# A fixed table for the opening of a windowed-attention and feed-forward kernel

## The chip, the cores and the metric

The kernel runs on one core of a Trainium2 chip. A core has five engines with queues of their own, which run at the same time and wait for one another through semaphores: TensorE (PE in the profile; PEld is its loading of weights), VectorE (DVE), ScalarE (ACT), GpSimd (POOL) and SyncE (SP, which here only issues DMAs). Every engine takes its instructions strictly in the order in which they stand in its queue. The metric is the device time of one execution in microseconds, the median of several runs. Lower is better.

## The reference

Two stages follow each other. The first is attention in a window over q, k, v of shape (8 batches, 8 heads, 576 positions, 64). The first four heads of a batch see the 32 latest positions, the other four every fourth of the 128 latest.

```python
scores = scale * np.matmul(q, k.transpose(0, 1, 3, 2))
mask_plain = (rel >= 0) & (rel < window)
mask_dil = (rel >= 0) & (rel < window * dilation) & (rel % dilation == 0)
scores = np.where(masks[None, :, :, :], scores, -1000000000.0)
scores = scores - np.max(scores, axis=-1, keepdims=True)
attn = np.exp(scores)
attn = attn / (np.sum(attn, axis=-1, keepdims=True) + 1e-09)
return np.matmul(attn, v).astype(np.float32)
```

Its result, seen as 4608 tokens by 512, goes through a feed-forward stage with weights 512 x 2048 and 2048 x 512.

```python
h = x @ w_in
relu6 = np.clip(h + 3.0, 0.0, 6.0)
g = h * relu6 / 6.0
return (g @ w_out).astype(np.float32)
```

All inputs are fp32, and the result is wanted to fp32's accuracy. So the kernel takes each fp32 operand of the feed-forward products apart into a rounded high part and a rest, and makes three products of them: high by high, high by rest, rest by high.

## The kernel before

**Attention in trios.** The work of the attention is cut into 48 trios. One trio is 192 positions of four heads, whose scores fill one 128x384 tile: every block of 32 queries meets only its own 32 keys and the 32 before it. The first 12 trios (two batches) are all done at the start and in a form of their own. For such a trio, TensorE adds the mask as a product (line 228) and 24 small score products (line 163, two passes each, so 48 matmuls in the trace); VectorE takes the row maxima and subtracts them (195, 196); ScalarE takes the exponential (200); TensorE turns the tile in three transposes (242), ScalarE copies it out of PSUM (245); TensorE multiplies by the values (line 173, again 48 matmuls), VectorE divides by the sums (207, 208, 210), TensorE turns again (242), ScalarE copies (247), and ScalarE and GpSimd write the high part xh (299) and the rest xl (302) of the feed-forward's input. The score products of a trio and the value products of the trio three before it are issued alternately, in one block of 96 matmuls. The other 36 trios are spread over the later feed-forward steps and turn by VectorE and DMAs.

**Feed-forward in steps.** The tokens are cut into 12 chunks of 384, the 2048 hidden units into 16 parts of 128. One step (chunk c, part f) is gemm1 (lines 397 to 418: 12 matmuls of 384 columns into a ps_h tile, then Relu, gate, high part and rest on ScalarE and VectorE in turn) and, two steps later, gemm2 (420 to 434: 9 matmuls of 512 columns into three ps_o tiles, which stay in PSUM while f runs). That makes 192 steps. Chunks 0 and 1 run interleaved so that each converted weight is used twice when it is new; LEAD says by how many steps chunk 0 is ahead.

**Weights.** The 16 parts come as 32 halves of 512 KB (an even half belongs to w_in, an odd one to w_out), and each is converted on the chip: two products on ScalarE (338, 339), three steps on VectorE (340, 346, 350), the high part on ScalarE (351), the rest on VectorE (355). The input says them as 64-bit words, hence the work on single bits. A pool of 18 slots of 8 KB per partition holds 16 converted parts, and in what is left the halves that are being converted; the inputs of trios 0 to 8 also lie there at first (the name first).

**What sets the order.** In the kernel before, the code hands work to a scheduler that orders each engine's queue, TensorE's too, by priorities and by a simulated time: step n has priority n, the evaluation of its first product n - 1.9, gemm2 n + 0.8, the rest between; constants such as CB, EARLY and WITH say beside which trio a conversion, a step or a load is handed over. SP's queue holds at most eight loads in flight: from the ninth on, each waits for the landing of the one eight before it.

Of the kernel before, what the change touches and what calls it, by code (L numbers as in the profile page):

```python
# [25 lines left out]
BEATS = 30  # L26
EXTRA = 2
WARM = 8
ONV = ()
AHEAD = 3  # L30
LEAD = 4
# [3 lines left out]
WITH = (0, 0, 0, 0, 2, 0, 2, 0, 2, 2, 2, 2)  # L35
CB = (6, 6, 7, 7, 8, 8, 9, 9, 10, 10, 11, 11, 12, 12)
BASE = 8
CD = 0.5
EARLY = (8, 9, 10, 11, 12, 13, 14, 15, 15)
# [3 lines left out]
NEG = -1.0e30  # L43


@with_exitstack
def windowed_attention_ffn(ctx: ExitStack, tc: tile.TileContext, qk, vp, w, mask, out):
# [73 lines left out]

    last = {}
    kqs, vs = {}, {}
# [11 lines left out]
    def load_qk(t):  # L135
        if t < T and t not in kqs:
            kqs[t] = load_tile(t, "kq", 0, KW + CH)
            nc.sync.dma_start(out=kqs[t], in_=qk[t].rearrange("h d x -> (h d) x"))
# [7 lines left out]
    es, ats, xs, xfs = {}, {}, {}, {}  # L146
    trios = _order(B)
# [10 lines left out]
    def mm_scores(t, ps, i, u, r, masked):  # L158
# [4 lines left out]
        last["pe"] = nc.tensor.matmul(  # L163
# [5 lines left out]
    def mm_values_first(t, ps, i, u, h):  # L169

        k, j = divmod(i, 2)
        rows, n, at, s = slice(j * D, (j + 1) * D), 4 * k + 2 * (1 - h) + u, QB * (2 * j + u), 2 * k + h
        last["pe"] = nc.tensor.matmul(
            ps[at : at + QB, s * W : (s + 1) * W],
            lhsT=ats[t][rows, QB * n : QB * (n + 1)], rhs=vs[t][rows, 4 * k + 2 * h + u, :], start=True, stop=True,
        )

    def mm_values(t, ps, i, u, r):

        rows, n, at = slice(r * D, (r + 1) * D), SLOTS * u + i, QB * (2 * (1 - r) + u)  # L180
        last["pe"] = nc.tensor.matmul(  # L181
# [4 lines left out]
    def softmax(t, ps, masked):  # L186
        e = work_tile("e")
        mx = small.tile([P, SLOTS], F32, name="mx")
        ev = e.rearrange("p (s x) -> p s x", x=2 * QB)
        sv = ps[:, :CH].rearrange("p (s x) -> p s x", x=2 * QB)  # L190
        if not masked:
            _, kind, part = trios[t]
            nc.vector.tensor_tensor(out=e, in0=ps[:, :CH], in1=mask_sb[:, 3 * kind + part], op=ALU.add)
            sv = ev
        nc.vector.tensor_reduce(out=mx, in_=sv, axis=AX.X, op=ALU.max)
        nc.vector.tensor_tensor(  # L196
            out=ev, in0=sv, in1=mx.rearrange("p (s o) -> p s o", o=1).broadcast_to([P, SLOTS, 2 * QB]),
            op=ALU.subtract,
        )
        nc.scalar.activation(e, e, AF.Exp, scale=SCALE)  # L200
        es[t] = e
        load_qk(t + NLOAD)

    def normalise(t, ps):
        pv = ps[:, : SLOTS * W].rearrange("p (s x) -> p s x", x=W)
# [9 lines left out]
        xs[t] = x  # L215
        load_v(t + NLOAD)
# [4 lines left out]
    def st_both(ts, tv):  # L221
# [7 lines left out]
        for i, u, r in blocks():  # L229
            if tv is not None:  # L230
                (mm_values_first if tv < NFIRST else mm_values)(tv, pv, i, u, r)
            if ts is not None:
                mm_scores(ts, ps, i, u, r, masked)
        if tv is not None:
            normalise(tv, pv)
        if ts is not None:
            softmax(ts, ps, masked)

    def turn(src, name):
# [3 lines left out]
        dst = work_tile(name)  # L243
        if name == "a":
            nc.scalar.copy(dst, ps[:, :CH])
        else:
            nc.scalar.copy(
                dst.rearrange("p (u i x) -> p i u x", u=2, x=QB),
                ps[:, :CH].rearrange("p (i u x) -> p i u x", u=2, x=QB),
            )  # L250
        return dst
# [18 lines left out]
    def st_turn_e(t, how):  # L270
        ats[t] = how(es.pop(t), "a")

    def st_turn_x(t, how):
        xfs[t] = how(xs.pop(t), "xf")

    def st_split(t):
        xf = xfs.pop(t)

        b, kind, part = trios[t]
        assert all(read[c] == NF for c in chunks(b - 2, kind, part))  # L280
        written.add((b, kind, part))
        xu = xf.rearrange("p (u f) -> p u f", u=2)
        half = CH // 2
        to = lambda x: x[:, 2 * kind : 2 * kind + 2, b % 2 * S : b % 2 * S + S]
        pieces = []
        if kind == 0:
            pieces.append((xu, lambda x: to(x)[:, :, half * part : half * (part + 1)]))
        else:
            at = half * part
            while at < half * (part + 1):  # L290
                c, i0 = divmod(at, CLS)
                n = min(CLS - i0, half * (part + 1) - at)
                pieces.append((
                    xu[:, :, at - half * part : at - half * part + n],
                    lambda x, c=c, i0=i0, n=n: to(x).rearrange("p u (i c) -> p u c i", c=DIL)[:, :, c, i0 : i0 + n],
                ))
                at += n
        for src, view in pieces:
            nc.scalar.copy(view(xh), src)  # L299
        for src, view in pieces:  # L300
            eng = nc.vector if t in ONV else nc.gpsimd
            eng.tensor_tensor(out=view(xl), in0=src, in1=view(xh).bitcast(F32), op=ALU.subtract)  # L302
# [3 lines left out]
    def pace(ins):  # L306

        if "pe" in last:
            tc.add_manual_dep(
                ins.ins, last["pe"].ins.name,  # L310
                mybir.DependencyInfo(mybir.DependencyClass.NoSync, mybir.DependencyReason.DATA), reason="pace",
            )
# [5 lines left out]
    wt, staged = {}, {}  # L318
    WN = w.shape[3]

    def load_w(p):
        st = wpool.tile([P, 4, WN], F32, name="st", tag="w")
        pace(nc.sync.dma_start(
# [4 lines left out]
    def parts(p):  # L328
        st = staged[p]
        f, j = divmod(p, 2)  # L330
# [284 lines left out]
```

## Time and profile before

| what | value |
|---|---|
| median of 3 runs | 915.96 us (915.54 to 918.5) |
| profiled execution | 915.34 us, of which its span is 913.57 us |
| TensorE busy over the span | 891.0 us, 98% |
| VectorE, ScalarE, GpSimd busy | 444.0, 346.5, 62.5 us |
| mean granted TensorE clock | 0.991 |
| first matmul of a feed-forward step starts | 34.2 us |
| TensorE without any gap | from 100.3 us to 909.0 us |

The span is the time from the first to the last instruction. In the profile a matmul's end is modelled and matmuls overlap, so a row's mean duration is longer than the distance at which such matmuls follow each other; distances are read from starts. "Idle before" is time in which the engine had nothing under way ahead of an instruction, with the instruction or DMA that ended it; "issue" stands there if nothing that the profile records ended it.

### The profile page before, as it was taken

Reading aid. Unit: us, or ns where it says so; the run is one execution under the profiler, and the core shown is the slowest. Engines: PE = TensorE matmul, PEld = TensorE weight load, DVE = VectorE, ACT = ScalarE, POOL = GpSimd, SP = SyncE. Lnnn points to the kernel's source line nnn. Section 1 sums busy time; section 2 is a strip of 40 time slices with the busy share of each in tenths; the row PEclk is TensorE's granted clock in tenths of the full one; section 3 lists DMA queues with packets and bytes.
Section 4 is the critical chain, followed back from the end, with each engine's and each line's share of the span. In section 5 each row is a group of like instructions: output and inputs, shape, how many; then the busy total and the mean of one; then the engine's idle time right before and its main releaser. Section 6 shows DMA issues by size and latency. Waiting matters only on the chain.

```text
span 913.6 us, 20574 instructions
## 1 busy us (share of the span) xinstructions
PE 891.0 (98%) x8732; PEld 791.6 (87%) x8732; DVE 444.0 (49%) x934; ACT 346.5 (38%) x661; POOL 62.5 (7%) x77
## 2 busy tenths in 40 slices
PE   6897999999999999999999999999999999999998
PEld 4576999989889899899888989988888998899996
DVE  3899983244545454444454445445444544422221
ACT  2778862333333333233333223233333332332322
POOL 0212100000010110000000000000100010000000
PEclk9799999999999999999999999999999999999999
DMA  9927430022313222222122123113211310100000
GB/s 354 386 83 260 140 93 0 1 95 89 86 54 119 72 70 81 66 67 84 47 85 85 48 64 104 51 46 99 71 49 52 116 32 11 45 5 1 36 1 34
DMA packets 37820, 74.87 MB, mean 82 GB/s; under 512 B 7264, under 2 KB 16608, under 8 KB 37728
## 3 DMA queue, kind: packets, MB, share of 16 engines
q1 hardware_dynamic: 32544, 64.12, 21.8%
q10 hardware_dynamic: 5184, 9.44, 2.7%
q8 instruction: 68, 1.11, 0.5%
q14 instruction: 24, 0.20, 0.1%
HBM read 57.02 MB, written 9.44 MB: 73 GB/s over the span
## 4 chain that ended last, share of the span: by engine, by line
PE 92%; DMA 4%; DVE 2%; ACT 1%; issue 0%; SPq 0%; POOL 0%
PE ps_o L428 15%; PE ps_h L407 15%; PE ps_h L409 14%; PE ps_h L408 14%; PE ps_o L429 14%; PE ps_o L430 14%; PE ps_a L181 3%; PE ps_a L163 2%; DMA first<-in_v 2%; DMA st<-in_w 1%; DMA v<-in_v 1%; DVE st L350 1%; DVE st L346 1%; DVE wt L355 0%; PE ps_a L242 0%
## 5 line engine op out<-in xcount | busy, mean ns | idle before, releaser
L413 DVE SCALAR_TENSOR_TENSOR t<-t,ps_h 128x384 f32<-128x384 f32 x192 | 106.3, 554 | 326.0 <-ACT t L412 325.8
L407 PE MATMUL ps_h<-xh,wt 128*128 128x384 f32 x768 | 261.5, 341 | 2.9 <-DVE t L413 2.8
L408 PE MATMUL ps_h<-xl,wt 128*128 128x384 f32 x768 | 259.9, 338 | 0.5 <-POOL xl L302 0.5
L409 PE MATMUL ps_h<-xh,wt 128*128 128x384 f32 x768 | 259.9, 338 | 0.0
L428 PE MATMUL ps_o<-wt,gh 128*128 128x512 f32 x576 | 228.7, 397 | 2.0 <-ACT gh L416 2.0
L429 PE MATMUL ps_o<-wt,gh 128*128 128x512 f32 x576 | 224.9, 390 | 0.0
L430 PE MATMUL ps_o<-wt,gl 128*128 128x512 f32 x576 | 221.3, 391 | 0.6 <-DVE gl L417 0.6
L412 ACT ACTIVATE t<-ps_h,three 128x384 f32<-128x384 f32 x192 | 111.1, 579 | 273.3 <-PE ps_h L409 273.0
L417 DVE TENSOR_TENSOR gl<-t,gh 128x384 fp32r<-128x384 f32 x192 | 107.0, 557 | 101.4 <-ACT gh L416 100.1
L407 PEld LDWEIGHTS ps_h<-xh,wt 128*128 128x128 f32 x768 | 144.9, 189 | 11.8 <-DVE t L413 3.3
L408 PEld LDWEIGHTS ps_h<-xl,wt 128*128 128x128 f32 x768 | 144.9, 189 | 8.7 <-POOL xl L302 0.6
L409 PEld LDWEIGHTS ps_h<-xh,wt 128*128 128x128 f32 x768 | 145.0, 189 | 0.8 <-issue 0.3
L416 ACT CAST gh<-t 128x384 fp32r<-128x384 f32 x192 | 98.5, 513 | 111.3 <-DVE t L413 109.1
L430 PEld LDWEIGHTS ps_o<-wt,gl 128*128 128x128 f32 x576 | 108.2, 188 | 24.2 <-DVE gl L417 1.0
L428 PEld LDWEIGHTS ps_o<-wt,gh 128*128 128x128 f32 x576 | 108.3, 188 | 20.1 <-ACT gh L416 2.3
L429 PEld LDWEIGHTS ps_o<-wt,gh 128*128 128x128 f32 x576 | 108.4, 188 | 15.7
L302 POOL TENSOR_TENSOR xl<-xf,xh 128x384 fp32r<-128x384 f32 (+3 forms) x72 | 62.2, 877 | 740.6 <-ACT xh L299 671.8
L200 ACT ACTIVATE e<-e 128x384 f32<-128x384 f32 x48 | 25.2, 526 | 112.4 <-DVE e L196 112.3
L163 PE MATMUL ps_a<-kq 64*32 64x64 f32 x1872 | 47.1, 225 | 0.0
L299 ACT CAST xh<-xf 128x384 fp32r<-128x384 f32 (+3 forms) x72 | 33.7, 536 | 34.7 <-DMA xf<-xf_t 34.6
L181 PEld LDWEIGHTS ps_a<-v,a 64*32 64x32 f32 x1728 | 35.8, 105 | 9.2 <-issue 8.6
L181 PE MATMUL ps_a<-v,a 64*32 64x65 f32 x1728 | 41.6, 225 | 0.0
(45 smaller groups left out, 494.6 us busy)
## 6 DMA issues: line engine op xcount, KB each, us to landing
st<-in_w SPq DMA_DIRECT2D x32, 512.0 KB, 5.7
kq<-in_qk SPq DMA_DIRECT2D x39, 416.0 KB, 4.5
v<-in_v SPq DMA_DIRECT2D x39, 390.0 KB, 3.5
out<-o ACTq DMA_DIRECT2D x36, 256.0 KB, 2.9
first<-in_qk SPq DMA_DIRECT2D x9, 416.0 KB, 8.0
first<-in_v SPq DMA_DIRECT2D x9, 390.0 KB, 8.5
a<-a_t SPq DMA_DIRECT2D x144, 24.0 KB, 1.8
xf<-xf_t SPq DMA_DIRECT2D x144, 24.0 KB, 1.8
```

Source lines behind the costliest of these rows:

```text
L163: last["pe"] = nc.tensor.matmul(ps[at : at + QB, 2 * QB * i : 2 * QB * (i + 1)], lhsT=x[rows, KW + QB * n : KW + QB * (n + 1)], rhs=x[rows ...
L181: last["pe"] = nc.tensor.matmul(ps[at : at + QB, i * W : (i + 1) * W], lhsT=ats[t][rows, QB * n : QB * (n + 1)], rhs=vs[t][rows, n, :], st ...
L407: nc.tensor.matmul(ph, lhsT=wt[f][:, 0, ks], rhs=a, start=(kt == 0), stop=False)
L408: nc.tensor.matmul(ph, lhsT=wt[f][:, 0, ks], rhs=b, start=False, stop=False)
L409: last["pe"] = nc.tensor.matmul(ph, lhsT=wt[f][:, 1, ks], rhs=a, start=False, stop=(kt == NK - 1))
L412: nc.scalar.activation(t, ph, AF.Relu, bias=three, scale=1.0)
L413: nc.vector.scalar_tensor_tensor(out=t, in0=t, scalar=6.0, in1=ph, op0=ALU.min, op1=ALU.mult)
L416: nc.scalar.copy(gh, t)
L417: nc.vector.tensor_tensor(out=gl, in0=t, in1=gh.bitcast(F32), op=ALU.subtract)
L428: nc.tensor.matmul(po[c][tt], lhsT=gh[:, ts], rhs=wt[f][:, 2], start=(f == 0), stop=False)
L429: nc.tensor.matmul(po[c][tt], lhsT=gh[:, ts], rhs=wt[f][:, 3], start=False, stop=False)
L430: last["pe"] = nc.tensor.matmul(po[c][tt], lhsT=gl[:, ts], rhs=wt[f][:, 2], start=False, stop=(f == NF - 1))
```

## The change

The opening (the first 12 trios, all 32 halves of weights, and the first 28 feed-forward steps) is no longer handed to the scheduler with priorities. Its operations are listed in a table of names, ORDER, and issued in that order on ScalarE, VectorE and SyncE; for TensorE the whole program is now issued in the order of the code. For this, the functions that did several engines' work are cut into one function for each operation, and a letter names each: B a block of products (scores of trio t, values of trio t - 3), V values alone, R maxima, S subtraction, X exponential, E and Y the two turnings, CA and CX their copies, Z the division, XH and XL high part and rest, U Q s j a h l the seven operations of converting a half, k v w M loads, G and H the two products of a step, RE T GH GL its evaluation.

Other parts of it: xl of the first 12 trios is made on VectorE (before: GpSimd). LEAD is 2 (before 4). The two products of a step are whole, with no other product between them. The step after which trio 12 begins lies one step later. After the table, steps are handed over as before, with the conversion taken out. Loads of k and v also stand inside S and Z (`load_qk(t + NLOAD)`, `load_v(t + NLOAD)`), so a load can be issued there before its own name comes up in the table.

```diff
-LEAD = 4
+LEAD = 2
...
+FOLLOW = 3
+ORDER = """
+M1 k0 M0 k1 w0 B0 k2 B1 R0 w2 S0 U0 R1 k3 X0 s0 Q0 B2 S1 v0 j0 X1 E0 U2 R2 v2 E1 CA0 a0 Q2 w4 S2 h0 s2 B3 X2 l0 k5
+CA1 j2 k7 E2 a2 CA2 Z0 k4 U4 Q4 R3 B5 v1 h2 s4 S3 k6 j4 X3 Y0 R5 E3 CX0 v3 Z2 CA3 B4 XH0 w1 S5 XL0 X5 k9 a4 Y2 E5 R4
+CX2 B6 v4 CA5 Z1 XH2 w5 S4 h4 Y1 XL2 U1 R6 w3 X4 CX1 Z3 E4 Q1 v5 S6 CA4 Y3 XH1 l4 B7 v6 X6 XL1 CX3 l2 U3 k8 E6 s1
...
+    def shifted(t):
+        sv, mx = pss.pop(t)
         nc.vector.tensor_tensor(
...
+            in1=mx.rearrange("p (s o) -> p s o", o=1).broadcast_to([P, SLOTS, 2 * QB]), op=ALU.subtract,
+        )
         load_qk(t + NLOAD)
...
-            eng = nc.vector if t in ONV else nc.gpsimd
+    def low(t, eng):
+        for src, view in pieces_of(t):
             eng.tensor_tensor(out=view(xl), in0=src, in1=view(xh).bitcast(F32), op=ALU.subtract)
...
+        "B": lambda t: block(t, t - FOLLOW if t >= FOLLOW else None),
+        "V": lambda t: block(None, t),
...
+        "XH": high, "XL": lambda t: low(t, nc.vector),
...
-    place(-5, lambda: st_both(NFIRST, None))
-    place(-3, lambda: st_turn_e(NFIRST, turn_by_blocks))
+    place(-3, lambda: st_both(NFIRST, None))
+    place(-1, lambda: ats.update({NFIRST: turn_by_blocks(es.pop(NFIRST), "a")}))
...
+    with tc.manual_schedule(
+        engines={mybir.EngineType.Activation, mybir.EngineType.DVE, mybir.EngineType.SP}
+    ):
+        for name in ORDER.split():
+            kind = name.rstrip("0123456789")
+            first_operations[kind](int(name[len(kind) :]))
...
-        windowed_attention_ffn(tc, *args, o)
+        with tc.manual_schedule(engines={mybir.EngineType.PE}):
+            windowed_attention_ffn(tc, *args, o)
```

Where the instructions now stand, at three places. First TensorE's queue at the first product of step 0. Before, the products of step 0 (ps_h, lines 407 to 409) stand one by one between value products (line 173) and score products (163) of a block:

```order
L242 MATMUL ps_a<-ident,x 128x128 x3
L228 LDWEIGHTS mi
L228 MATMUL ps_a<-mi 128x384
L407 MATMUL ps_h<-xh,wt 128x384
L173 MATMUL ps_a<-first,a 32x65
L408 MATMUL ps_h<-xl,wt 128x384
L163 MATMUL ps_a<-first 32x64
L409 MATMUL ps_h<-xh,wt 128x384
L173 MATMUL ps_a<-first,a 32x65
L407 MATMUL ps_h<-xh,wt 128x384
L163 MATMUL ps_a<-first 32x64
```

Now (line 187 is a score product, 197 a value product, 285 a transpose, 432 to 434 the first product of a step):

```order
L197 MATMUL ps_a<-first,a 32x65
L187 MATMUL ps_a<-first 32x64
L285 MATMUL ps_a<-ident,e 128x128 x3
L432 MATMUL ps_h<-xh,wt 128x384
L433 MATMUL ps_h<-xl,wt 128x384
L434 MATMUL ps_h<-xh,wt 128x384
L432 MATMUL ps_h<-xh,wt 128x384
L433 MATMUL ps_h<-xl,wt 128x384
```

The 12 matmuls of step 0 stand together, behind the blocks of trios 0 to 9; before, they began in the block of trio 8's scores and were spread over that one and the next.

Second, SyncE's queue of loads at the values of trios 4 and 6 (first_106 and first_112 before, first_203 and first_365 now; st is a half of weights, kq the queries and keys of a later trio). Before:

```order
L138 DMA first_112<-in_qk 128x832
L144 DMA first_106<-in_v 128x780
L323 DMA st_115<-in_w 128x1024
L323 DMA st_117<-in_w 128x1024
L138 DMA first_119<-in_qk 128x832
L144 DMA first_109<-in_v 128x780
L138 DMA first_122<-in_qk 128x832
L144 DMA first_112<-in_v 128x780
```

Now:

```order
L161 DMA first_365<-in_qk 128x832
L167 DMA first_229<-in_v 128x780
L371 DMA st_442<-in_w 128x1024
L161 DMA first_445<-in_qk 128x832
L161 DMA kq_449<-in_qk 128x832
L167 DMA first_203<-in_v 128x780
L371 DMA st_526<-in_w 128x1024
L371 DMA st_540<-in_w 128x1024
L167 DMA first_365<-in_v 128x780
```

The values of trio 4 are the 22nd load (the 14th before), those of trio 6 the 25th (the 20th before); the first halves of weights have gone ahead of them, as have the values of trio 5 (first_229) and the keys of trios 8 and 9.

Third, the making of xl. Before, on GpSimd:

```order
L302 TENSOR_TENSOR xl<-xf,xh 128x2x192 x2
L302 TENSOR_TENSOR xl<-xf,xh 128x2x144
L302 TENSOR_TENSOR xl<-xf,xh 128x2x48
L302 TENSOR_TENSOR xl<-xf,xh 128x2x96 x2
L302 TENSOR_TENSOR xl<-xf,xh 128x2x48
```

Now in VectorE's queue, between the conversion of weights (393, 413), the softmax (219, 224) and the division (236 to 239):

```order
L224 TENSOR_TENSOR e<-ps_a,mx 128x384
L413 TENSOR_TENSOR wt<-st,wt 128x512
L343 TENSOR_TENSOR xl<-xf,xh 128x2x192
L413 TENSOR_TENSOR wt<-st,wt 128x512
L393 TENSOR_SCALAR st<-st 128x512
L236 TENSOR_SCALAR z<-ps_a 128x6
L237 RECIPROCAL z<-z 128x6
L239 TENSOR_TENSOR x<-ps_a,z 128x384
L219 TENSOR_REDUCE mx<-ps_a 128x6
L343 TENSOR_TENSOR xl<-xf,xh 128x2x96 x2
```

The 18 operations of the first 12 trios have moved from GpSimd to VectorE; those of the other 36 trios are still on GpSimd.

More of the change, by code (lines that the diff above doesn't have):

```diff
@@ L119, in windowed_attention_ffn, with in_turn @@
     nc.gpsimd.memset(three, 3.0)
+    kqs, vs = {}, {}
     last = {}
-    kqs, vs = {}, {}
+    def in_turn(ins):
+        for name in last.values():
+            tc.add_manual_dep(
+                ins.ins, name, mybir.DependencyInfo(mybir.DependencyClass.NoSync, mybir.DependencyReason.DATA), reason="in turn"
+            )
     wide = {}
@@ L268, in turn_by_blocks, with pieces_of @@
         return dst
[L270 to L277, printed above, removed]
+    def pieces_of(t):
+        b, kind, part = trios[t]
+        xu = xfs[t].rearrange("p (u f) -> p u f", u=2)
+        half = CH // 2
+        to = lambda x: x[:, 2 * kind : 2 * kind + 2, b % 2 * S : b % 2 * S + S]
+        if kind == 0:
+            return [(xu, lambda x: to(x)[:, :, half * part : half * (part + 1)])]
+        found, at = [], half * part
+        while at < half * (part + 1):
+            c, i0 = divmod(at, CLS)
+            n = min(CLS - i0, half * (part + 1) - at)
+            found.append((
+                xu[:, :, at - half * part : at - half * part + n],
+                lambda x, c=c, i0=i0, n=n: to(x).rearrange("p u (i c) -> p u c i", c=DIL)[:, :, c, i0 : i0 + n],
+            ))
+            at += n
+        return found
@@ L279, in st_split, with high @@
+    def high(t):
         b, kind, part = trios[t]
         assert all(read[c] == NF for c in chunks(b - 2, kind, part))
[L281 to L297, printed above, removed]
@@ L298, in st_split @@
-        for src, view in pieces:
+        for src, view in pieces_of(t):
             nc.scalar.copy(view(xh), src)
-        for src, view in pieces:
-            eng = nc.vector if t in ONV else nc.gpsimd
+    def low(t, eng):
+        for src, view in pieces_of(t):
             eng.tensor_tensor(out=view(xl), in0=src, in1=view(xh).bitcast(F32), op=ALU.subtract)
[L306 to L312, printed above, removed]
@@ L318, in windowed_attention_ffn, with st_split @@
-    wt, staged = {}, {}
+        xfs.pop(t)
+        written.add(trios[t])
+    def st_split(t):
+        high(t)
+        low(t, nc.gpsimd)
+    steps = [(0, f) for f in range(LEAD)]
+    for f in range(NF):
+        if f + LEAD < NF:
+            steps.append((0, f + LEAD))
+        steps.append((1, f))
+    steps += [(c, f) for c in range(2, NCH) for f in range(NF)]
+    when = {f: steps.index((0, f)) for f in range(NF)}
+    wt, staged, converted = {}, {}, set()
     WN = w.shape[3]
@@ L482, in step_at @@
             step()
-        turn_of(n + 0.4)
-        if LEAD <= n < BEATS:
-            convert_beat()
         turn_of(n + G2)
-        if n >= LAG:
-            gemm2(*steps[n - LAG])
+        if n - LAG not in done:
+            gemm2(n - LAG)
         turn_of(n + DEL + 0.5)
```

283 lines of the change are left out of this document (136 added, 147 removed).

## The prediction

> **What bounds the kernel now.** I read the span on the page first, then busy time by stage, then the groups of TensorE's instructions up to 100.28 us, then what TensorE waits for.
>
> ```profile
> span 913.6 us, 20574 instructions
> ...
> 50.60:100.30 49.70, 44.35 (x549) 36.80 (x550) 49.19 (x97) 42.50 (x86) 11.44 (x10) 0.97 0.56 189
> 100.30:909.10 808.80, 808.71 (x7318) 729.17 (x7316) 365.50 (x776) 277.24 (x525) 43.08 (x54) 1.00 0.19 59
> ...
> L407 PE MATMUL ps_h<-xh,wt 128*128 128x384 f32 x36 | 14.3, 401 | 2.9 <-DVE t L413 2.8
> ...
> L428 PE MATMUL ps_o<-wt,gh 128*128 128x512 f32 x21 | 8.9, 423 | 2.0 <-ACT gh L416 2.0
> ```
>
> The rows of the stages are busy us of PE, PEld, DVE, ACT, POOL with counts, then clock, DMA share and GB/s. From 100.3 us on TensorE is never idle at full clock, and the change leaves that work as it is: there is nothing to gain behind 100.3 us. TensorE's queue is the same there but for the place of a block by part of a product; only trio 12 is turned one step, 4.1 us, ahead of its values, against two before, for which two turnings on VectorE (under 1 us) and a transfer of 1.8 us (rows below) leave room; without it, 1 us at most. The last two rows are of the first 100.28 us: 36 matmuls of line 407 at 4 a step and 21 of line 428 at 3 a step are 9 first and 7 second products, beside the 12 trios. In 50.6 to 100.3 us VectorE is busy for 49.19 of 49.70 us, so it sets the pace there. What sets the first 50 us is in TensorE's waits:
>
> ```profile
> PE ps_a L173 <- issue: 9.3, 4, 3.8
> ...
> 31.98 0.21 PE L173 MATMUL ps_a<-first,a 64*32 64x65 f32 x1 [3.42 <-issue]
> ...
> 13.30:19.60 6.30, 2.47 (x127) 1.96 (x127) 1.75 (x5) 1.00 (x2) 0.00 (x0) 0.98 1.03 410
> 19.60:25.80 6.20, 5.34 (x126) 4.12 (x127) 3.50 (x10) 2.85 (x7) 1.00 (x1) 0.74 1.03 406
> 25.80:31.90 6.10, 2.69 (x127) 2.17 (x127) 4.73 (x11) 4.72 (x10) 1.00 (x1) 1.00 1.03 406
> ...
> q8 instruction: 68, 1.11, 0.5%
> ```
>
> Four times, 9.3 us in all and 3.8 at the longest, TensorE waits for "issue", which is nothing recorded; the wait that ended at 31.98 us is one. The next rows are three stretches from one such wait's end to the next. From each such wait to the next lie 127 matmuls and 127 weight loads, some 254 instructions, and 6.1 to 6.3 us, while the DMA engines are full (share 1.03). The instruction queue carries 68 packets, 1.11 MB: 16 KB each. I read this as a refill of TensorE's instructions: on entering one block of some 255 the next is sent for, and with the load stream full it comes 6.2 us later.
>
> **Prices of TensorE's work.**
>
> ```profile
> 57.32 0.81 PE ps_a L242 x6
> ...
> 108.03 0.68 PE ps_o L430 x3
> 112.15 0.68 PE ps_o L430 x3
> ...
> 349.21 0.43 PE ps_o L428
> ...
> 367.07 0.43 PE ps_o L428
> ...
> 64.17 0.34 PE L228 MATMUL ps_a<-mi 128*128 128x384 bf16 x1
> 64.44 0.26 PE L163 MATMUL ps_a<-kq 64*32 64x64 f32 x4
> ```
>
> From the chain of waits (start, us; the last two rows are TensorE's timeline): a step takes 112.15 - 108.03 = 4.12 us, 2.06 for each product. Four steps and a later trio take 17.86 us, so a block of 96 small matmuls is 17.86 - 16.5 = 1.35 us. Three transposes are 0.4 us, the mask 0.27 us (64.17 to 64.44). A block of scores and values is then 1.62 us, scores alone about 1.0, values alone 0.75.
>
> **When step 0 can begin.** In the table, the scores of trios 0 to 9 and the values of trios 0 to 6 come ahead of G0. Two paces meet there. First the loads:
>
> ```profile
> 10.22 8.35 DMA first<-in_v
> ...
> 18.58 9.14 DMA st<-in_w
> ...
> st<-in_w SPq DMA_DIRECT2D x32, 512.0 KB, 5.7
> ...
> v<-in_v SPq DMA_DIRECT2D x39, 390.0 KB, 3.5
> ...
> first<-in_qk SPq DMA_DIRECT2D x9, 416.0 KB, 8.0
> first<-in_v SPq DMA_DIRECT2D x9, 390.0 KB, 8.5
> ...
> xf<-xf_t SPq DMA_DIRECT2D x144, 24.0 KB, 1.8
> mi<-in_mask SPq DMA_DIRECT2D x1, 384.0 KB, 6.6
> mi<-in_mask SPq DMA_DIRECT2D x1, 224.0 KB, 2.7
> ```
>
> From the chain, then the DMA issues with KB each and us to landing. Before, the 14th load is issued at 10.22 us, when the 6th has landed, and lands 8.35 us later; the 22nd is issued at 18.58 and lands at 27.72 us. By the KB of the rows, 2246, 5470 and 9130 KB have come by 10.20, 18.57 and 27.72 us. By the new order, v0 ends at 4102 KB (15.0 us), k5 at 5420 KB (18.4), v1 at 6616 KB (21.4), v4 at 9156 KB (27.8), v6 at 10570 KB (at 400 KB/us, 31.3). By loads alone the block of trio 9's scores and trio 6's values begins at 31.3, the next follows, and G0 stands 1.62 + 1.62 + 0.4 later, at 35.0 us.
>
> Second the refills. Each matmul counts twice (its weight load): warm-up 16, scores alone 98, a block 194, three transposes 6. Block ends lie at about 190, 446, 702, 958, 1214, 1470 and 1726; G0 begins at 1748. Walking the table, with 6.2 us from entering a block to having the next:
>
> - 190, in B1 (k1 ends at 1440 KB, about 8.1 us), is passed at 9.1; the next block is there at 15.3.
> - 446 lies in B3, which waits for v0 until 15.0; passed at 15.9, next there at 22.1.
> - 702 lies at the end of B5 (k5, 18.4); reached at 19.7, waits to 22.1; next at 28.3.
> - 958 is early in B6; 3.6 us of B4 and turnings bring it to 25.8; waits to 28.3; next at 34.5.
> - 1214 is a third into B7; reached at 31.5; waits to 34.5; next at 40.7.
> - 1470 lies in B9; reached at 38.0 (Y4 waits for the division); waits to 40.7.
> - 1726 ends B8, reached at 42.9. The loads issued without a wait (to v8, 13596 KB) have ended at 38.9 us, since the next one waits for B9; so this refill meets an empty stream. No row prices that; it lies between 1.8 us (a 24 KB transfer's landing) and 6.2. I take 3.0, nearer the transfer: 43.7.
>
> So G0 begins at 44.2 us, set by the refills and not by the loads.
>
> The Trainium skill's page "Runtime: NRT & Kernel Launch", section Instruction fetch mechanics, also says blocks of 256 instructions in 16 KiB, the next fetched while one runs, and calls a crossing mostly hidden. The trace agrees on the block, and with waits of up to 3.8 us not on the hiding; by the page's rule the 35.0 us above would hold, the first rival.
>
> **The sum.** Behind the start of G0, TensorE has left of the 12 trios B10 and B11 (2 x 1.62), three value blocks (3 x 0.75) and 11 turnings (11 x 0.4): 9.9 us. Then 9 + 7 products, 16 x 2.06 = 33.0 us, bring it to where it stood before at 100.3 us, and 913.6 - 100.3 = 813.3 us follow. 44.2 + 9.9 + 33.0 + 813.3 = 900.4 us without a stall. What the interleaving of step 0's products with small ones cost before goes with the old 50.6 us and needs no term.
>
> Stalls behind G0. A refill passed at 43.7 is wanted at the end of B10, while loads run again: 0.8 us. VectorE is the larger question:
>
> ```profile
> 72.26 0.16 DVE L207 TENSOR_SCALAR z<-ps_a 128x6 f32<-128x6 f32 x1
> ...
> 72.72 0.18 DVE L208 RECIPROCAL z<-z 128x6 f32<-128x6 f32 x1
> ...
> 73.50 0.43 DVE L340 TENSOR_SCALAR st<-st 128x512 uint32<-128x512 uint32 x1
> 73.84 0.68 DVE L350 CUSTOM_DVE_ANT_0 st<-st 128x1024 uint16<-128x1024 uint16 x1
> 74.44 1.44 DVE L346 SCALAR_TENSOR_TENSOR st<-st 128x512 uint32<-128x512 uint32 x1
> ...
> 74.15 2.04 POOL L302 TENSOR_TENSOR xl<-xf,xh 128x288 fp32r<-128x288 f32 x2 [12.19 <-ACT xh L299]
> ...
> 79.14 0.68 DVE L346 SCALAR_TENSOR_TENSOR st<-st 128x512 uint32<-128x512 uint32 x1
> 79.74 0.54 DVE L413 SCALAR_TENSOR_TENSOR t<-t,ps_h 128x384 f32<-128x384 f32 x1
> 80.20 0.68 DVE L355 TENSOR_TENSOR wt<-st,wt 128x512 fp32r<-128x512 f32 x1
> ```
>
> From start to start, the shift takes 0.34 us, the other operations on 512 elements 0.60, those on 384 0.46, the two small ones of a division 0.34 together. An xl moved here costs about 0.5 us a trio, 6 us in all. But beside GpSimd's xl (74.15 us) line 346 took 1.44 us instead of 0.68, and if each of the 18 pieces has cost VectorE between nothing and 0.76 us, the move gives back up to 14. I take zero, between -8 and +6. From XL4 to G7 the table holds for VectorE 25 operations on 384 (11.5), 15 on 512 (9.0), 6 shifts (2.0) and 7 divisions (5.6): 28.1 us. TensorE has from G0 to G7 ten products (20.6), two blocks, three value blocks and 11 turnings (9.9): 30.5. VectorE can start about 1.5 us sooner, so some 4 us of room stand against every wait in a fixed order, behind which the whole of its queue waits: the gates of the next steps, and behind those TensorE. I allow 3 us of stall, between 0 and 15. Weights: a late half's load waits for the slot that another half's conversion frees, and needs 3.5 us (v's median, nearest in size on an idle stream) or some more to land; the table has it used no sooner, so I add nothing (rival 3 is the other end). ScalarE and SyncE get no term: by the page ScalarE is busy 38% and the loads up to the tenth half go out without a wait for conversion.
>
> The clock:
>
> ```profile
> 33.00:43.30 10.30, 10.30 (x117) 6.90 (x117) 9.13 (x18) 7.81 (x16) 3.12 (x4) 0.50 1.03 405
> 91.10:94.50 3.40, 3.40 (x13) 3.21 (x12) 3.40 (x8) 2.15 (x5) 1.54 (x1) 0.50 0.90 339
> ...
> 90.00 0.44 PE L407 MATMUL ps_h<-xh,wt 128*128 128x384 f32 x1 [2.82 <-DVE t L413]
> ```
>
> After the waits of 3.42 us (to 31.98) and 2.82 us (to 90.00) the granted clock was 0.50 for 10.3 and 3.4 us. The walk above has waits of 2.4 to 3.0 us up to 40.7, so a half-rate stretch over G0 is likely: 1.7 us (half of 3.4), at most 5.1.
>
> 900.4 + 0.8 + 3.0 + 1.7 = 905.9 us of span. The profiled run took 915.34 with a span of 913.57, 1.7 more; it lies 0.6 under the median. So **907.5 us**, 0.9% faster.
>
> **Rivals.**
>
> 1. Refills are hidden, loads alone set the start. For it: in the stretch to 25.80 us TensorE was busy for 5.34 of 6.20 us, so there the refill came almost in time; against it: three stretches of the same 6.2 us, two of them with TensorE busy less than half. G0 at 35.0 and no 0.8: 907.5 - 10 = 897.5 us.
> 2. VectorE's fixed order binds. For it: 49.19 of 49.70 us before, and 4 us of room only. Of the table's 121 us for it (32 x 2.14 for the halves, 56 x 0.46 for the gates, 12 x 2.2 for the trios) some 99 lie behind XL4. If the waits in its queue add 15% to these, 15 us, the 4 us of room take off a part and TensorE is 11.5 us late instead of 3: 916 us, no change.
> 3. Slower: the slots of the weights. LEAD 2 leaves fewer parts in hand. The last 13 halves wait for a freed slot; one round of load (3.5), two products, four VectorE steps and a copy is 3.5 and some 4 us, with two slots 3.75 us a half against the 4.12 in which TensorE uses one. A round of 10.6 us costs 1.2 us a half, 15 us over 13 halves in place of VectorE's 3: 919 us, and from there on it is slower than before. Against it: the table has a round of 8 to 10 us there, and TensorE two steps in hand. I put it at 921.
> 4. The half clock lasts its long form over the first steps: 3.4 us more, 911. The Trainium skill's page "TensorE: Matmul & The Clock Gate", Part 1, has the rate back after some 3.4 us of busy time. The 10.3 us row disagrees.
>
> **How the numbers follow.** Forecast (902 to 912) 0.56; rival 1 0.14; rival 2 0.14; rival 3 0.09; rival 4 0.07. A measurement of this kernel can tell 0.3%, 2.7 us, from no change: faster means below 913.2, slower above 918.7. Faster: 0.55 + 0.14 + 0.05 + 0.02 = 0.76; same 0.13 (most of rival 2, edges); slower 0.11 (rival 3, the tail of 2). The range reaches to rivals 1 and 2: 897 to 916; the forecast's own is 902 to 912.
>
> **What would show it.** Right: TensorE's "issue" waits of 2 to 3 us about 254 instructions apart at roughly 20, 26, 32 and 38 us; the first matmul of line 432 at 43 to 46 us; from there waits of TensorE under 6 us; gap-free from about 90 us; the tail as long as before. Wrong: line 432 first at 35 us (rival 1); waits on VectorE or ScalarE of over 10 us between 45 and 100 us (rival 2); ScalarE waiting for st loads behind 100 us with TensorE idle after (rival 3).

## The result and the profile after

The changed kernel takes 906.13 us (median of 4, 905.96 to 908.97) against 916.97 us (median of 4, 915.54 to 918.5) for the kernel before on the same chip: ratio 0.9889, 95% interval 0.9861 to 0.9916. The forecast was 907.5 us in a range of 897 to 916. The profiled execution took 908.97 us, the longest of the four, with a span of 907.2 us; so 6.4 us of the 10.8 are seen in the two traces.

Two stretches show where they lie. In the kernel before, 9 first and 7 second products and all of the 12 trios are done at 100.29 us; in the changed one, 10 first and 6 second products, as much work, at 92.32 us. Busy time by stage (columns as in the prediction), the changed kernel first, then the kernel before:

```profile
0.00:92.32 92.32, 75.76 (x1419) 62.76 (x1420) 67.22 (x149) 59.32 (x121) 0.30 (x5) 0.87 0.72 258
92.32:903.10 810.78, 809.01 (x7315) 728.65 (x7314) 382.02 (x804) 286.36 (x540) 43.00 (x54) 1.00 0.20 62
```

```profile
0.00:100.29 100.29, 82.31 (x1415) 62.40 (x1416) 78.53 (x159) 68.21 (x136) 19.45 (x23) 0.91 0.71 263
100.29:909.10 808.81, 808.72 (x7318) 729.17 (x7316) 365.51 (x776) 277.25 (x525) 43.08 (x54) 1.00 0.19 59
```

The opening is 7.97 us shorter. TensorE's idle time fell only from 17.98 to 16.56 us in it; the larger part, 6.55 us, is busy time, for the same matmuls and at a lower mean clock (0.87 against 0.91). Behind the opening the changed kernel gives 1.97 us back. What TensorE waited for most, in total, times and the longest, in the changed kernel:

```profile
PE ps_a L197 <- issue: 9.0, 5, 3.5
PE ps_a L187 <- DMA first<-in_qk: 1.9, 3, 1.0
PE ps_a L197 <- ACT a L290: 1.8, 2, 1.4
```

The issue waits are as long as before (9.0 against 9.3 us), and no wait for VectorE's or ScalarE's gates is left behind G0 (the first product of step 0; H is a second product). The places, from TensorE's timeline:

```profile
22.82 0.31 PE L197 MATMUL ps_a<-first,a 64*32 64x65 f32 x1 [2.45 <-issue]
...
29.31 0.21 PE L197 MATMUL ps_a<-first,a 64*32 64x65 f32 x1 [0.26 <-issue]
...
35.56 0.31 PE L197 MATMUL ps_a<-first,a 64*32 64x65 f32 x1 [2.29 <-issue]
...
43.47 0.24 PE L197 MATMUL ps_a<-first,a 64*32 64x65 f32 x1 [0.46 <-issue]
...
44.12 0.42 PE L432 MATMUL ps_h<-xh,wt 128*128 128x384 f32 x1
...
52.42 0.26 PE L197 MATMUL ps_a<-first,a 64*32 64x65 f32 x1 [3.54 <-issue]
...
208.48 0.24 PE L205 MATMUL ps_a<-v,a 64*32 64x65 f32 x1 [1.43 <-DMA a<-a_t]
```

G0 stands at 44.12 us, forecast at 44.2. The last row but one is the refill at the end of B10, the last one a wait at trio 13's values, far behind the opening.

**Where the busy time went.** The form behind an instruction's name, 128*128 or 64*32, is that of TensorE's array. Feed-forward products, transposes and the mask are 128*128, score and value products 64*32. Rows of TensorE's timeline (start, us, then duration, us), in the kernel before:

```profile
44.29 0.44 PE L409 MATMUL ps_h<-xh,wt 128*128 128x384 f32 x1
44.66 0.30 PE L173 MATMUL ps_a<-first,a 64*32 64x65 f32 x2
44.89 0.44 PE L407 MATMUL ps_h<-xh,wt 128*128 128x384 f32 x1
```

and in the changed kernel:

```profile
65.98 0.34 PE L433 MATMUL ps_h<-xl,wt 128*128 128x384 f32 x1
66.15 0.34 PE L434 MATMUL ps_h<-xh,wt 128*128 128x384 f32 x1
66.32 0.34 PE L432 MATMUL ps_h<-xh,wt 128*128 128x384 f32 x1
```

From start to start, a wide product behind its like costs 0.17 us; one wide and two small products cost 0.60, and the two small ones are worth about 0.02 us each in a block (48 in 0.9 us). So a turn, from wide to small and back, costs 0.39 us. Along the timelines TensorE turns from 128*128 to 64*32 32 times before 100.29 us in the kernel before, and 14 times before 92.32 us now: 18 x 0.39 = 7.0 us, about the 6.55 us of busy time. The traces say the same when all distances from start to start are added up, idle time left out: the products before and behind a change of form take 17.8 us in the kernel before (64 of them) and 7.5 us now (28). The 36 fewer have a price of their own of 18 x (0.17 + 0.02) = 3.4 us, which leaves 6.9 us. The run "between" below puts turns back.

The Trainium skill's page "TensorEngine Tiling (Array Packing)", section Key Properties, says that a change of the tiling mode, not only of the tile, drains TensorE. The rows agree as far as they go: the small products start 0.37 us behind the wide one (44.29 to 44.66), where another wide one would start after 0.17. The loads of weights show a second thing. At a turn, a wide product's load starts together with it (both at 44.89 in the kernel before), while behind its like the load starts 0.17 us ahead of its product (66.15 against 66.32 in the changed kernel):

```profile
44.89 0.19 PEld L407 LDWEIGHTS ps_h<-xh,wt 128*128 128x128 f32 x1
```

```profile
66.15 0.19 PEld L432 LDWEIGHTS ps_h<-xh,wt 128*128 128x128 f32 x1
```

How much of the 0.39 us is draining and how much is this load, which has nothing to hide behind, no run here separates.

### The profile page after: what moved, and what is told of

The parts are those of the page before. It is cut to its first block, busy times and chain, and to the rows that moved or that the text cites. A ratio compares the mean times of both kernels' runs of the same rounds, so it can differ in the third digit from the quotient of the medians.

```text
span 907.2 us, 20562 instructions
## 1 busy us (share of the span) xinstructions
PE 884.8 (98%) x8732; PEld 791.4 (87%) x8732; DVE 449.2 (50%) x952; ACT 346.2 (38%) x661; POOL 43.3 (5%) x59
## 4 chain that ended last, share of the span: by engine, by line
PE 94%; DMA 2%; issue 1%; DVE 1%; SPq 1%; ACT 1%
PE ps_o L462 15%; PE ps_h L432 15%; PE ps_h L433 14%; PE ps_h L434 14%; PE ps_o L464 14%; PE ps_o L463 14%; PE ps_a L205 3%; PE ps_a L187 2%; PE ps_a L197 1%; DMA first<-in_qk 1%; PE ps_a L285 1%; DMA st<-in_w 1%; DMA a<-a_t 1%; SPq L311 0%; PE ps_a L260 0%
## 5 line engine op out<-in xcount | busy, mean ns | idle before, releaser
L464 PE MATMUL ps_o<-wt,gl 128*128 128x512 f32 x576 | 224.6, 390 | 0.0
L446 ACT CAST gh<-t 128x384 fp32r<-128x384 f32 x192 | 98.5, 513 | 103.0 <-DVE t L442 100.3
L343 POOL TENSOR_TENSOR xl<-xf,xh 128x384 fp32r<-128x384 f32 (+3 forms) x54 | 43.0, 807 | 753.9 <-ACT xh L339 499.2
```

What stands on the lines that cost most here:

```text
L446: nc.scalar.copy(ghs[n], ts[n])
L464: nc.tensor.matmul(po[c][tt], lhsT=gl[:, rows], rhs=wt[f][:, 2], start=False, stop=(f == NF - 1))
```

## The experiments

Times are medians, each beside the kernel before on the same chip: 916.15 us in the first group, 916.52, 916.3 and 915.36 us in the others. The changed kernel (906.13 us) was measured beside a kernel before of 916.97 us, so small differences from it are better read from the ratios to the kernel before; its own is 0.9889 (0.9861 to 0.9916).

### Putting turns back: between

```diff
+                between.append(one) if n in (1, 3) else one()
...
         for nth, (i, u, r) in enumerate(blocks()):
+            if nth % 2 == 0 and between:
+                between.pop(0)()
```

> The changed kernel with the 12 products of G1 put one by one between the small products of B11, and those of G3 between those of V11, as the kernel before had them; nothing else is moved. Theory S (each turn from small products to a 384-column product and back costs 0.3 to 0.4 us, as in the trace of before at 44.1 to 46.5 us): 24 turns cost 7 to 9 us, and the time is 913 to 915.5 us. Rival (the gain came from the order as such, or from xl on VectorE, and turns are free): 906 to 907 us.

Measured: 923.03 us (919.09 to 928.03, six executions), ratio to the kernel before 1.0079 (1.0046 to 1.0113), so slower than before. The first product of step 3 with the 48 small ones of V11, in stretches of this run and then of the changed kernel:

```profile
71.07:79.99 8.92, 8.92 (x65) 5.35 (x61) 3.47 (x9) 3.05 (x6) 0.00 (x0) 0.95 0.16 47
```

```profile
65.70:68.90 3.20, 3.20 (x65) 2.86 (x61) 3.13 (x8) 3.20 (x7) 0.00 (x0) 1.00 0.48 140
```

The same 60 matmuls (65 rows with the edges) take 8.92 us instead of 3.20. There are 12 turns where the changed kernel has one, so 5.7 us for 11 more, 0.52 us each, the last 0.9 us of the stretch at half clock. At full clock the timeline of this run shows a little less:

```profile
71.07 0.45 PE L437 MATMUL ps_h<-xh,wt 128*128 128x384 f32 x1
71.44 0.41 PE L197 MATMUL ps_a<-v,a 64*32 64x65 f32 x4
71.78 0.44 PE L437 MATMUL ps_h<-xl,wt 128*128 128x384 f32 x1
```

From one wide product to the next, with four small ones between, it is 0.71 us, which is 0.46 us over their own 0.17 + 4 x 0.02. The profiled execution (920.59 us) ends TensorE's work 11.6 us later than the changed kernel's; the 22 turns more make 10 to 11 us of that. Theory S holds in its mechanism, with a price that had been put too low. The size of the loss is not all explained, as the median lies 16.9 us above the changed kernel's. The six executions spread over 9 us, and their mean clock goes with it (0.990 in the fastest, 0.976 and 0.978 in the two slowest); why the clock is lower in them is not settled.

### Undoing turns alone: b_code

```diff
-        windowed_attention_ffn(tc, *args, o)
+        with tc.manual_schedule(engines={mybir.EngineType.PE}):
+            windowed_attention_ffn(tc, *args, o)
```

> The kernel before with one part of the change alone: TensorE's queue in the order of the code, so that the products of a step stand whole; ScalarE, VectorE, SyncE and GpSimd are ordered as before. Theory S (turns between small and wide products cost 0.39 us in the trace of before and 0.44 to 0.47 in the run with products between): the 25 turns go, 7 to 10 us, new waits take back up to 3, and the time is 906 to 912 us, G9 as early as 90 to 96 us (before 100.3). Rival (the table's order of the other engines made the gain): 915 to 918 us.

Measured: 919.67 us, ratio 1.0033 (1.0019 to 1.0047): slower than before, and outside both ranges. Up to 100 us turns fell from 32 to 15, but TensorE's waits are now:

```profile
PE ps_a L173 <- issue: 10.9, 5, 4.0
PE ps_a L242 <- ACT a L245: 4.6, 1, 4.6
PE ps_h L407 <- ACT xh L299: 4.4, 2, 3.0
PE ps_h L408 <- POOL xl L302: 2.0, 2, 1.3
```

The idle time up to 110 us rose from 18.0 to 26.1 us. New are waits for ScalarE (4.6 us for a copy in front of a transpose, 4.4 us for xh in front of whole products) and for GpSimd's xl (2.0 us). The mean clock is lower too, 0.981 to 0.985 in the six executions against 0.985 to 0.990 in the kernel before beside them. So I read the turns of the kernel before as the price of filling waits: its small products stood where TensorE would have waited. In the changed kernel the table puts whole products where their inputs are ready, on all engines. Issuing TensorE's work in the order of the code gains nothing without the table. What the table would do with the old TensorE order was not run, beyond the two products of "between", nor was LEAD or the place of trio 12 varied alone.

### Are refills what sets G0: tiny64

```diff
+    for _ in range(64):
+        nc.tensor.matmul(idle[:32, :16], lhsT=zeros[:64, :32], rhs=zeros[:64, P : P + 16], start=True, stop=True)
```

> The changed kernel with 64 tiny products of zeros more (128 instructions of TensorE, half a block of a refill) behind the warm-up, in the 1.7 us in which TensorE waits for the mask; they are of no use to the result. Theory R (refills set the start): every refill is reached half a block of work sooner, the issue waits in front of G0 lengthen by about 3 us, G0 begins at 46 to 47.5 us and the time is 908 to 909.5 us. Rival (the loads or the chain of operations set the start): G0 stays at 44.1 us and the time at 906.

Measured: 906.91 us (905.7 to 907.12). Waits, then the start of G0 on TensorE's timeline:

```profile
PE ps_a L199 <- issue: 6.2, 4, 1.9
PE ps_a L287 <- issue: 2.0, 2, 1.3
```

```profile
47.19 0.42 PE L434 MATMUL ps_h<-xh,wt 128*128 128x384 f32 x1
```

G0 moved by 3.07 us, half of 6.2, though the 64 products lie in idle time. Ahead of it, the issue waits at block ends finish at 21.08, 27.36, 33.66 and 39.90 us on TensorE's timeline, 6.2 to 6.3 us apart, so the forecast's mechanism for G0 is shown. The clock differs as well, 0.50 from 12.7 to 46.9 us in this execution, but TensorE waited at each of these block ends, and the shift is already 3.29 us right behind the last of them (a transpose at 40.25 us against 36.96). The time moved by 0.8 us instead of 2 to 3, which the spread of the executions does not tell from nothing. With the block ends 128 instructions earlier none falls into B10 any more; that wait of 3.54 us is gone, and G1 stands at 52.95 us against 54.68. What one refill costs, the next one's place gave back.

### How long a refill takes: depth4 and quiet

depth4 makes every load wait for the one four before it:

```diff
+        if DEPTH <= len(sent) < 45:
+            tc.add_manual_dep(
+                ins.ins, sent[-DEPTH], mybir.DependencyInfo(mybir.DependencyClass.Sync, mybir.DependencyReason.DATA), reason="few in flight"
+            )
+        sent.append(ins.ins.name)
```

> The changed kernel, in which each of the first 45 loads waits for the landing of the load four before it (now eight). Theory R (a refill of TensorE's instructions waits behind the loads in flight): with half as many in flight a refill takes some 3 us instead of 6.2, the issue waits fall from 9.0 us to 3 or less, G0 begins at 38 to 41 us instead of 44.1 and the time is 901 to 904 us. Rival L (the refill's pace has nothing to do with the loads): the issue waits stay near 9 us and the time near 906 us. A third end: four loads in flight do not fill the load stream (in the changed kernel 193 GB/s were moved between 43.5 and 53.8 us), G0 waits for loads and comes after 46 us, and the time is over 908 us.

Measured: 905.09 us (904.62 to 906.86), above the forecast 901 to 904. That is 1.0 us under the changed kernel, but the ratio to the kernel before is the same (0.9887 against 0.9889). Its waits, and the stretch from 20 to 30 us:

```profile
PE ps_a L207 <- issue: 3.7, 4, 1.9
PE ps_a L207 <- DMA first<-in_v: 3.0, 1, 3.0
```

```profile
20.00:30.00 10.00, 8.38 (x259) 6.68 (x242) 7.03 (x19) 5.56 (x14) 0.00 (x0) 0.69 0.98 341
```

The issue waits fell from 9.0 to 3.7 us, but the stream moved 341 GB/s (404 in the changed kernel), and G0 came at 42.53 us, not at 38 to 41. The packets of the instruction queue show the mechanism: up to 33 us, they start 3.2 to 3.9 us after TensorE enters the block before the one that they bring in the changed kernel, and 1.5 to 2.5 us after it with four loads in flight. So with more loads in flight a refill goes out later. That G0 gained only 1.6 us says that other work is nearly as late as the refills: TensorE now waits 3.0 us for the values of a trio (the second row).

quiet moves loads away from the stretch in which B10's refill is fetched:

```diff
-        load_qk(t + NLOAD)
+        if t != 9:
+            load_qk(t + NLOAD)
...
-        load_v(t + NLOAD)
+        if t != 7:
+            load_v(t + NLOAD)
```

and in the table v10, v11, w10 and w9 stand behind Z9, k12 behind w12, U10 ahead of Q10.

> The changed kernel with the loads of v10, v11 and the weight halves 10 and 9 behind v12's, which waits for the end of V9, and k12's behind the weight half 12; so from about 41 us to the end of V9 no load is in flight (in the changed kernel five are). The products of half 10 on ScalarE begin later by the same. Theory R (a refill waits behind the loads in flight): the block that TensorE waits for in B10 (3.5 us up to 52.42 in the changed kernel, 2.2 us up to 50.80 in the run with trio 13 turned) comes in under 3 us, that wait is under 0.5 us, G1 begins at 49 to 50.5 us and the time is 902.5 to 904.5 us. Rival: the wait there is not set by loads; G1 stays at 52 to 54.7 us and the time at 906. Third end: v10, v11 or a half come late, TensorE waits for them at V10 or G5, and the time is 906 to 910 us.

Measured: 910.42 us (908.21 to 911.07), nearest to the third end and just above its 906 to 910, though TensorE did not wait where that end had it. From 41.9 to 52.5 us next to nothing was moved, and B10's refill cost 0.81 us:

```profile
41.90:52.50 10.60, 9.22 (x295) 7.83 (x278) 7.66 (x20) 5.21 (x12) 0.00 (x0) 0.86 0.01 3
```

```profile
51.48 0.21 PE L197 MATMUL ps_a<-first,a 64*32 64x65 f32 x1 [0.81 <-issue]
```

Against theory R, however, this block took its full 6.2 us (from 45.27, where TensorE entered the one before, to 51.48) with no load in flight, and not under 3; TensorE has 5.4 us of work meanwhile, which leaves 0.8. In the changed kernel, with five loads in flight, the same block took 8.95 us (43.47 to 52.42). The packets show where the time goes: this refill's starts 3.9 us after TensorE enters the block before it (45.27 to 49.15) with nothing in flight, which is as late as under a full stream up to 33 us, and 6.5 us after it (43.47 to 49.92) in the changed kernel. So loads may lengthen it, but they are not all of it; what delays it in an empty stream is not settled. G1 came at 52.78 us, since G0 had begun later (45.93). The price of the later loads is ScalarE's wait for a half of weights, behind which TensorE waited 2.6 us for an exponential:

```profile
60.24 0.66 ACT L391 ACTIVATE st<-st 128x512 uint32<-128x512 uint32 x1 [4.13 <-DMA st<-in_w]
```

### Room on VectorE and the move of xl: dve_more and xl_pool

dve_more runs line 450 twice in the steps 0 to 7, with the same values:

```diff
+        t = ts.pop(n)
+        for _ in range(1 + (MORE if n < 8 else 0)):
+            nc.vector.tensor_tensor(out=gls[n], in0=t, in1=ghs[n].bitcast(F32), op=ALU.subtract)
```

> The changed kernel; in each of the steps 0 to 7 VectorE makes the rest of the gate twice (8 operations on 384 more, about 0.5 us each, 4 us in all; the second writes the same values). Theory of the prediction (VectorE has some 4 us of room up to G7): no new wait, 906 to 907 us. Rival V (VectorE, busy for 28.62 of the 29.8 us from 62.2 to 92 us, just keeps up): TensorE waits for gates between G3 and G9, G9 comes 3 to 4 us later and the time is 909 to 910 us.

Measured: 907.66 us (906.69 to 908.77). For 4 us more on VectorE, TensorE waited 1.2 us, in G8 for a converted weight and once for a gate:

```profile
PE ps_h L435 <- DVE wt L414: 1.0, 1, 1.0
...
PE ps_h L433 <- DVE t L443: 0.2, 1, 0.2
```

From the start of G2 to that of G10 this run took 38.95 us (56.54 to 95.49) and the changed kernel 36.92 (59.48 to 96.40), so 2.0 of the 4 us came through. The truth lies between the two: some 2 us of room, less than the forecast's 4, but enough that the changed kernel lost nothing there. In the changed kernel VectorE was busy for 28.62 of 29.80 us, and TensorE still never waited for it:

```profile
62.20:92.00 29.80, 29.80 (x245) 26.90 (x244) 28.62 (x59) 24.83 (x50) 0.00 (x0) 1.00 0.53 177
```

xl_pool puts xl back on GpSimd:

```diff
-        "XH": high, "XL": lambda t: low(t, nc.vector),
+        "XH": high, "XL": lambda t: low(t, nc.gpsimd),
```

> The changed kernel with xl of the first 12 trios back on GpSimd. The prediction put this move at nothing (6 us of VectorE's time against the slowing of VectorE beside GpSimd). By that: 905.5 to 907 us, with pieces on GpSimd of some 2 us and operations of VectorE on 512 elements beside them of 1.4 us instead of 0.68. Rival (GpSimd's pieces are longer and stand in the chain to G0 and to the first steps of chunk 1, some 1.5 us at XL4 and more at XL11): G0 at 45.5 us or later and 907.5 to 910 us. Other rival (VectorE gains 6 us that TensorE waited for): under 905 us.

Measured: 907.08 us (905.26 to 909.91), G0 at 43.55 us. No difference that can be told, as forecast. The group of GpSimd's pieces of 384 from 25 to 100 us (busy us, mean ns):

```profile
L343 POOL TENSOR_TENSOR xl<-xf,xh 128x384 fp32r<-128x384 f32 x6 | 6.4, 1060 | 41.5 <-ACT xh L339 41.5
```

One of them, and VectorE's sign step (line 399) beside it (start, duration, us):

```profile
47.81 1.15 POOL L343 TENSOR_TENSOR xl<-xf,xh 128x384 fp32r<-128x384 f32 x1 [5.94 <-ACT xh L339]
```

```profile
48.14 1.37 DVE L399 SCALAR_TENSOR_TENSOR st<-st 128x512 uint32<-128x512 uint32 x1
```

A piece of 384 takes 1.06 us (the 2.04 us of the row of before were two pieces of 288). The forecast's price for VectorE is borne out where the two meet: this sign step took 1.37 us, and the other five of the six from 25 to 80 us 0.68. But they seldom meet: from 25 to 100 us five operations of VectorE beside a piece are lengthened, by 2.9 us in all, against up to 14 in the forecast.

### The loss at 208 us: trio13

```diff
-        place(p + 1, lambda t=t: xfs.update(...))
+        place(p + (2 if i == 0 else 1), lambda t=t: xfs.update(...))
...
-            place(p + 2, lambda t=t: ats.update(...))
+            place(p + (1 if i == 0 else 2), lambda t=t: ats.update(...))
```

> The changed kernel; behind trio 12's values the exponentials of trio 13 are turned ahead of trio 12's result (now behind it). Theory: the 1.43 us wait of TensorE at 208.5 us comes from trio 13's turned values standing behind the four transfers of trio 12's result in the queue of loads; it goes, and the time is 904.5 to 905 us. Rival: trio 13 is late because its scores are, and the wait stays or moves behind trio 12's result: 906 us.

Measured: 904.29 us (904.06 to 905.55), ratio 0.9877 (0.9861 to 0.9893). By the ratios that is 1.1 us under the changed kernel, with intervals that overlap; the place of the gain is seen in the traces. SyncE's issues in the changed kernel, and then in this run:

```profile
200.50 2.42 SPq L311 DMA_DIRECT2D xf<-xf_t  x4
203.02 2.42 SPq L311 DMA_DIRECT2D a<-a_t  x4
```

```profile
197.52 2.43 SPq L311 DMA_DIRECT2D a<-a_t  x4
200.05 3.30 SPq L311 DMA_DIRECT2D xf<-xf_t  x4
```

Trio 13's turned values go out at 197.52 us in this run, ahead of trio 12's result; in the changed kernel they went at 203.02 behind it. The wait of 1.43 us is gone; 0.26 us at trio 12's values stay. The theory holds. In the kernel before, the products with trio 13's values began at 215.60 us, 16.96 us behind trio 12's (198.64); in the changed kernel, in the order of the code, they begin 14.4 us behind them (192.34 to 206.72), too soon for four transfers queued behind four others.

### Towards a faster version: v0_early, v0_early_d6, v0_early_d4, trio13_d4

v0_early builds on trio13: in the table w2 stands behind v0, U2 behind CA0, and S1 no longer issues k4. The next two limit the loads in flight to six and to four; the last one is trio13 with four. Of the table's edit, a piece of one line:

```diff
-S1 v0 j0 X1 E0 U2 R2 v2 E1 CA0
+S1 v0 w2 j0 X1 E0 R2 v2 E1 CA0 U2
```

> The run with trio 13 turned in the other order (904.29 us), with the load of v0 ahead of weight half 2's and of k4's (k4 comes behind trio 0's division), and the product of half 2 on ScalarE behind the copy of trio 0's exponentials. TensorE waited 2.84 us for v0, to 15.34 us, in the run with trio 13 turned. Theory R (from there on the refills, one every 6.2 us, set the start): v0 lands some 2 us sooner, the block behind 450 is entered as much sooner, every later refill comes 1.5 to 2 us sooner, G0 begins at 42 to 42.5 us (43.88) and the time is 902.3 to 903 us. Rival (k4, half 2 or another load is late in its place and the later refills are not tied to the first): G0 at 43.5 us or later, 904 to 905 us.

> The run with v0 early, with at most six loads in flight (eight). With four in flight a refill was sent 1.5 to 2.8 us after TensorE entered a block, with eight 3.6 to 3.9 us, but the load stream fell from about 405 to 342 GB/s. Theory R: with six the refill is sent after some 2.8 to 3 us and a block takes 5.3 us instead of 6.2, the stream stays above 380 GB/s, G0 begins 1.5 to 3 us sooner than with eight, at 39.5 to 41 us, and the time is 901 to 902 us. Rival (what a faster refill gains, a slower stream takes back): within 0.7 us of the run with v0 early.

> The run with v0 early, with at most four loads in flight. The run with four in flight alone was 1.0 us faster than the changed kernel (905.09 against 906.13). If the three steps add up: 906.13 - 1.0 - 1.8 - 1.5 to 2, some 901.5 us. Rival (with four in flight the loads, at 342 GB/s, set the start, not the refills, so v0's place no longer moves G0): 903 to 904 us.

> The two edits that were faster than the changed kernel (906.13 us), together: trio 13 turned in the other order (904.29 us alone) and at most four loads in flight (905.09 us alone). They act at different places, 43 to 51 us and 208 us. If the gains add up: 906.13 - 1.8 - 1.0, 903.3 us, with TensorE's issue waits near the 3.7 us of the run with four in flight and no wait over 0.3 us behind 200 us. Rival (what four in flight gained lies within the spread of the half-clock stretches from run to run, as the 906.47 us of the run with v0 early and four in flight suggests): 904 to 905 us, no better than trio 13 alone.

Measured: 906.31 (904.14 to 907.87), 904.74 (902.68 to 906.4), 906.47 (904.76 to 907.64) and 904.36 us (903.7 to 905.93), with ratios of 0.9887, 0.9869, 0.9888 and 0.9875. No theory of a gain held; only trio13_d4 lies in its rival's range, and the other three times lie outside both of theirs. In v0_early the wait for v0 is gone, but TensorE waits for an exponential instead, and the later refills end little sooner or not at all (34.04 and 43.18 us; 34.69 and 43.22 in trio13):

```profile
17.53 0.33 PE L286 MATMUL ps_a<-ident,e 128*128 128x128 f32 x1 [1.86 <-ACT e L232]
```

G0 lies at 43.84, 43.36 and 43.15 us in the first three. Together with depth4 (42.53) this suggests that two paces, refills and the chain of loads and operations, run within 1 to 2 us of each other up to G0, so that easing one is worth little. trio13_d4 is no faster than trio13 alone. trio13 has the lowest median, 1.2% under the kernel before; its ratio is not to be told from those of v0_early_d6, trio13_d4 and the changed kernel.

## Why the prediction was right, and where not

The time (907.5 forecast, 906.13 measured) and the mechanism of the start (refills set G0) were right. What made the gain, the turns, the prediction did not name, and single terms behind G0 were off and cancelled each other, which is luck: a refill 2.7 us too small, a stall 3.0 us too large. Against the profiled execution, the longest of the four (2.8 us above the median):

| step of the prediction | forecast | measured |
|---|---|---|
| G0 begins | 44.2 us | 44.12 us |
| refill at the end of B10 | 0.8 us | 3.54 us |
| VectorE's fixed order | 3.0 us | no wait |
| half clock | 1.7 us, over G0 | some 1.4 us, over B10's rest and G1 |
| as much work done as before at 100.3 us | 44.2 + 9.9 + 33.0 + 0.8 + 3.0 + 1.7 = 92.6 us | 92.32 us |
| behind it | 813.3 us | 907.2 - 92.32 = 814.9 us |
| span | 905.9 us | 907.2 us |

- **The walk to G0** forecast issue waits to 22.1, 28.3, 34.5, 40.7 and 43.7 us; they ended at 22.82, 29.31, 35.56, not at all near 40.7, and 43.47. tiny64 shows that the refills carry it. Rival 1 (refills hidden, G0 at 35.0) is excluded by these rows. But the walk took the refills as the only pace: depth4 and v0_early show another one close behind.
- **Interleaving "needs no term".** The unit prices came from whole products and undisturbed blocks, so the sum held the gain of the turns without naming it. It is some 6.5 of the 8 us of the opening. The reading that VectorE sets the pace from 50.6 to 100.3 us missed this: 11 of the 32 turns lie in that stretch, booked as TensorE's busy time. Nor does a full VectorE (28.62 of 29.80 us in the changed kernel) make TensorE wait.
- **The refill at the end of B10** is the term that was mis-sized most. It was put at 6.2 us from 43.7; it took 8.95 in the changed kernel, while five loads were in flight, and 6.2 with none; what sets it there is open.
- **VectorE's stall** of 3 us did not come: dve_more finds some 2 us of room instead of 4, and that was enough. Rival 2 (waits of 10 us and more for VectorE) falls by the waits of the profile after. The move of xl at zero agrees with xl_pool, within the spread of its executions (905.26 to 909.91 us).
- **The clock.** The price was right, the place was not. Between 44.10 and 52.40 us the clock was 0.98; the half rate came behind the wait of 3.54 us:

```profile
52.12:55.53 3.41, 3.11 (x61) 2.94 (x61) 2.14 (x7) 0.46 (x2) 0.00 (x0) 0.50 0.14 20
```

  From that refill to G2 the changed kernel needed 7.06 us (52.42 to 59.48), trio13, which had full clock there, 5.69 (50.80 to 56.49). Rival 4 (a long form over the first steps) did not come in this execution.
- **Trio 12, "1 us at most"**, was too small and at the wrong trio. Its own values waited for 0.26 us; trio 13's, 1.43. The step of the prediction that failed here is "TensorE's queue is the same there but for the place of a block by part of a product": the distance between the two trios' values had shrunk by 2.6 us.
- **Rival 3 (slots of weights)**: no wait of TensorE for weights stands in the profile after.

## What to carry to other kernels

Count how often TensorE changes the form of its array, not only how long it is idle: here 0.4 to 0.5 us a turn were hidden in busy time, and filling a wait with a small product cost about as much as the wait. Whole products paid only together with an order on the other engines that has their inputs ready (b_code against the changed kernel). And a stretch dense in small matmuls was paced by the fetching of instructions: where a block ends decides where the wait falls (tiny64). Shorter issue waits alone bought nothing that can be told (depth4: 3.7 us instead of 9.0, at the same ratio).

## What the runs showed of the hardware that was not expected

- A turn of TensorE from 128*128 to 64*32 products and back costs 0.39 us with two small products between (before), and 0.46 us with four (between).
- With eight loads in flight the packet of a refill (16 KB) starts 3.2 to 3.9 us after TensorE enters a block, with four 1.5 to 2.5 us. Once, with nothing in flight, the packet still started 3.9 us after it and the block took 6.2 us to come; this is open.
- Four loads of 390 to 512 KB in flight moved 341 GB/s (depth4, 20 to 30 us), eight 404 (the changed kernel, the same stretch).
- One VectorE step on 512 elements beside a GpSimd subtraction of 384 took 1.37 us, alone 0.68 (xl_pool).
- The stretches of half clock lie elsewhere in each profiled execution of the same opening (52.12 to 55.53 us in the changed kernel, 36.4 to 43.2 in trio13), and one over G1 costs some 1.4 us; executions of one kernel spread by 1.5 us and more, which is of this size.
